# Chunk attention and a multiplicative FFN on one core: q and k of the first two tiles loaded four tokens a partition and transposed by 64 columns

## The chip, the core and the metric

The kernel runs on one core of one Trainium2 chip. TensorE (PE) does matmuls and transposes into PSUM; VectorE (DVE) and ScalarE (ACT) copy and do the softmax; GpSimd (POOL) issues the loads that cast float32 to bf16 on the way; SyncE (SP) issues the transposes by DMA and the transfers of the output. All transfers share 16 DMA engines. The metric is the device time of one execution in microseconds, the median of several runs.

## What is computed

```python
# q, k, v: (8, 8, 576, 64) float32; chunks of 64 tokens, 9 per batch, 8 heads
scores = (1 / sqrt(64)) * matmul(q_c, k_c.transpose(0, 1, 2, 4, 3))   # 64 x 64 in each chunk
attn = exp(scores - scores.max(-1)); attn /= attn.sum(-1) + 1e-9
x = matmul(attn, v_c)                        # heads side by side: (4608, 512)
h = ((x @ w1) * (x @ w2)) @ w3               # d_model 512, d_ff 1024
out = h @ w_out                              # (4608, 512) float32
```

## The kernel before

A group is 128 tokens, two chunks, of all 8 heads; 36 groups make the 4608 tokens. A tile is four groups, 512 tokens; there are nine. w3 and w_out are first multiplied to one matrix, w3o (`add_w3o`: eight times eight transposes, L448, and eight matmuls, L459), so that a tile is x by w1 and w2 (L491), the product of both (DVE, L500), and that by w3o (L522).

A group (`add_group`, L324) goes: load of q and k (`load_qk`, L267: one transfer each, 128 tokens on 128 partitions, 8 heads of 64 numbers, so runs of 256 bytes in HBM and 128 bytes in SBUF); transpose of both, for groups 0 to 11 by eight PE transposes of 128 columns (`t_emit`, L337), for groups 12 to 35 by one DMA transpose (`qk_turn`, L341); copies of k to `kT` and of q to `qd`, whose other half is zero, so that one matmul does two heads (L229 on ACT, L231 on DVE); eight score matmuls (L365) into `p_sc`; maximum, difference, exponential, sum and normalisation (L373, L377, L381, L385, L391); transpose of the result by PE (`at_emit`, L396) or, for groups 16 to 35, by a DMA transpose (`at_turn`, L347); eight matmuls with v (`av_emit`, L407) into `p_av`; a copy into `xt` (`x_copy`), from which L491 reads.

The order of all work is set by `Plan`: every operation is added with its engines, a cost, a key and what it needs, and a list scheduler picks, engine by engine, what is ready with the lowest key. The result is a fixed order for each engine, which the chip then follows; engines wait for one another on semaphores. Where the plan sees PE idle in the beginning, it puts dummy matmuls (`warm`, L585, 14 of them ahead of the first work). Loads are issued by POOL in the order of `LOADS`, then the other groups in turn. A transfer waits until the one eight places before it in its queue has landed. `ident`, which every PE transpose reads, is made by POOL at its place in `LOADS`, after eight loads and the first of the next.

SP issues, in the planned order, four staged rows of w_out, the DMA transposes, and the output: one transfer for each 128 tokens, 256 KB (`o_out`, L532). The output is held back until the loads of group 35 are in (`after=[c] + raws[OUT_AFTER]["ops"]`), with keys from `OUT_KEY` on; until then it lies in `kept`, parts of w3 and w_out that are no longer read, and in 20 buffers `o_sb`. So SP's queue reads, near the end: the DMA transpose of q and k of group 35, four outputs, that of the attention of group 32, eight outputs, group 33, five, group 34, six, group 35, the rest.

Of the kernel before, what the change touches and what calls it, by code (L numbers as in the profile page):

```python
# [10 lines left out]
ACT = mybir.ActivationFunctionType  # L11
# [3 lines left out]

LOADS = [('qk', 0), ('w3', 7, 8), ('w3', 3, 4), ('qk', 1), ('w3', 0, 1), ('wo', 4, 8), ('w3', 1, 2), ('ident',),
         ('qk', 2), ('w3', 2, 3), ('w3', 5, 6), ('qk', 3), ('w3', 6, 7), ('qk', 5), ('qk', 4), ('v', 0, 0, 2), ('w3', 4,
         5), ('w12', 0, 2), ('qk', 6), ('w12', 4, 6), ('qk', 7), ('w12', 2, 4), ('w12', 6, 8), ('qk', 8), ('v', 1, 0, 2),  # L20
         ('qk', 9), ('qk', 10)]
TILES = [4] * 9
XT = 16
STAGED = 4
OUT_AFTER, OUT_KEY = 35, 80
# [134 lines left out]
def kernel(  # L160
# [19 lines left out]
    nc = tc.nc  # L180
    B, H, S, D = q.shape
    C = 64
    NCH = S // C
    N_TOK = B * S
    D_MODEL = H * D
# [9 lines left out]
    bf = mybir.dt.bfloat16  # L195
    f32 = mybir.dt.float32

    BUFS = {"raw": 6, "kqT": 4, "kT": 3, "qd": 3, "vd": 3, "sd": 2, "e": 2, "an": 4, "at": 6, "w3t": 2, "abT": 2,
            "a_sb": 3, "o_sb": 20, "xt": XT, "ffn": 6, "p_sc": 1, "p_av": 1}
# [19 lines left out]

    qds = [wpool.tile([P, 2, NM, 2 * C], bf, tag=f"qd{i}", name=f"qd{i}") for i in range(BUFS["qd"])]  # L220
    vds = [wpool.tile([P, NM, NCH, 2 * D], bf, tag=f"vd{i}", name=f"vd{i}") for i in range(BUFS["vd"])]
    es = [wpool.tile([P, 8, C + 1], bf, tag=f"e{i}", name=f"e{i}") for i in range(BUFS["e"])]
    halves = [slice(0, C), slice(C, P)]

# [25 lines left out]
    def load(cost, issue, emit, **kw):  # L250
        return plan.add("POOL", cost, 0, emit, lag=landing, issue=issue, **kw)

    def chunks(g):
        return [divmod(2 * g + cc, NCH) for cc in range(2)]

    raws, v_got, v_first, w12_got, w3_got, wo_got, wo_cut = {}, {}, {}, {}, {}, [], []

    def load_qk(g):
        (b0, c0), (b1, c1) = chunks(g)
        parts = [(slice(0, P), b0, c0, 2)] if b0 == b1 else [(halves[0], b0, c0, 1), (halves[1], b1, c1, 1)]  # L260
        box = raws[g] = {"ops": []}
        for w, src in enumerate((q, k)):
            for r, b, c, n in parts:
                def emit(eng, w=w, src=src, r=r, b=b, c=c, n=n):
                    if "t" not in box:
                        box["t"] = sb("raw", [P, 2, H, D])
                    nc.gpsimd.dma_start(box["t"][r, w], src[b, :, c * C:(c + n) * C, :].rearrange("h p d -> p h d"))  # L267
                box["ops"].append(load(0.45 * n, 0.5 + 0.2 * n, emit, takes=() if box["ops"] else ("raw",)))

    def load_v(b, y0, y1):  # L270
        for t in range(2):
# [52 lines left out]

    def add_group(g, kt, ks, ka, kv):
        box = {}
        bc = chunks(g)
        qd = qds[g % len(qds)]

        turned = g in QK_BY_DMA  # L330

        def t_emit(eng):
            t = box["tr"] = ps("ffn", [P, 2, NM, P], bf)
# [23 lines left out]
            return emit  # L357

        def s_emit(eng):
            sc = box["sc"] = ps("p_sc", [P, 2, 2, 2, C])  # L360
# [7 lines left out]
        def flat(x):  # L368
            return x.rearrange("p cc y t k -> p (cc y t) k")

        def max_emit(eng):
            nm = box["nm"] = sb("nm", [P, 8, 1], f32, bufs=3)
            nc.vector.tensor_reduce(nm[:, :, 0], flat(box["sc"]), axis=AX.X, op=ALU.max)  # L373

        def sub_emit(eng):
            sd = box["sd"] = sb("sd", [P, 8, C], f32)
            nc.vector.tensor_sub(sd[:], flat(box["sc"]), box["nm"].to_broadcast([P, 8, C]))  # L377

        def exp_emit(eng):
            e = box["e"] = es[g % len(es)]  # L380
# [32 lines left out]
        got = raws[g]["ops"]  # L413
        if turned:
            tr = kc = plan.add("SP", 1.75, kt, qk_turn, after=got, takes=("kqT",), uses=[(got[0], "raw")], lag=3.5, issue=1.3)
            held, cost = [(tr, "kqT")], (0.35, 0.6)
        else:
            tr = plan.add("PE", 0.46, kt, t_emit, after=got + [made_ident], takes=("ffn",), uses=[(got[0], "raw")], lag=0.2)
            held, cost = [(tr, "ffn")], (0.43, 0.66)
            kc = plan.add(("DVE", "ACT"), cost, kt, k_copy, after=(tr,), takes=("kT",), uses=held)  # L420
        q0 = plan.add(("DVE", "ACT"), cost, kt, q_copy(0), after=[tr] + zero_q, takes=("qd",), uses=held)
        q1 = plan.add(("DVE", "ACT"), cost, kt, q_copy(1), after=(tr, q0), uses=held)
        s = plan.add("PE", 0.24, ks, s_emit, after=(kc, q0, q1), takes=("p_sc",), uses=[(kc, "kqT" if turned else "kT"), (q0, "qd")],
                     lag=0.2)
# [10 lines left out]
        av = plan.add("PE", 0.24, kv, av_emit, after=[ac] + [o for b, _ in bc for y_ in (0, 1) for o in v_got[b, y_]], takes=("p_av",),  # L435
                      uses=[(ac, "at")] + [(v_first[b], "vd") for b in sorted({b for b, _ in bc})], lag=0.2)
        x_done[g] = plan.add(("ACT", "DVE"), 0.68, kv, x_copy, after=(av,), takes=("xt",), uses=[(av, "p_av")])


    w3o_done = []  # L440
# [34 lines left out]
    outs = []  # L475
    kept = [w3_sb[:, i:i + 1, :].rearrange("p a n -> p (a n)").bitcast(f32) for i in range(FO)]
    kept += [wo_sb[:, i:i + 2, :].rearrange("p a n -> p (a n)").bitcast(f32) for i in range(0, FO, 2)]

    def add_tile(g0, n, kab, ko_):
        box = {}  # L480
# [32 lines left out]
        for tk, x0, x1 in cols:  # L513
            cuts = (0, FO - 2, FO) if last and not tk else (0, FO)

            def o_mm(i, tk=tk, x0=x0, x1=x1, cuts=cuts):
                def emit(eng):
                    if not i:
                        box["o", tk, x0] = ps("ffn", [P, D_MODEL])
                    t = box["o", tk, x0]  # L520
                    for ki in range(cuts[i], cuts[i + 1]):
                        nc.tensor.matmul(t[:, :x1 - x0], box["abT"][:, ki, tk * P:(tk + 1) * P], w3o_sb[:, ki, x0:x1],  # L522
                                         start=(ki == 0), stop=(ki == FO - 1))
                return emit

            def o_copy(eng, tk=tk, x0=x0, x1=x1):
                box["os", tk, x0] = kept[g0 + tk] if g0 + tk < len(kept) else sb("o_sb", [P, D_MODEL], f32)
                copy(eng, box["os", tk, x0][:, :x1 - x0], box["o", tk, x0][:, :x1 - x0])

            def o_out(eng, tk=tk, x0=x0, x1=x1):  # L530
                r0 = (g0 + tk) * P
                nc.sync.dma_start(out[r0:r0 + P, x0:x1], box["os", tk, x0][:, :x1 - x0])  # L532
# [15 lines left out]
    for what, *args in LOADS:  # L548
        if what == "ident":
            made_ident = plan.add("POOL", 0.6, 0, lambda eng: make_identity(nc, ident[:]), lag=0.3)  # L550
        else:
            {"qk": load_qk, "v": load_v, "w12": load_w12, "w3": load_w3, "wo": load_wo}[what](*args)
    landing = 2.5
    for g in range(NG):
        if g not in raws:
# [62 lines left out]
```

## Time and profile before

Three runs took 251.49, 253.83 and 252.03 us, median 252.03. The profiled execution took 252.69 us by itself, with a span of 250.9 us and a mean granted TensorE clock of 0.993.

| engine | busy us | share | what it does most |
|---|---|---|---|
| PE | 239.3 | 95% | L491 131.6, L522 66.8, L459 15.6 |
| DVE | 173.8 | 69% | L500 48.7, five softmax steps of about 24.5 each |
| ACT | 146.3 | 58% | copies 42.0 (`a_sb`), 22.7 (`qd`), exponential 22.8 |
| POOL | 101.4 | 40% | issue of loads |

The engines' busy times overlap, so they do not add up. The time line of an engine gives the start and length of a run of equal instructions, and in brackets the idle time ahead of it with what ended it. Matmuls are pipelined: the distance from one start to the next says what one costs, not the length. The DMA share in the stretches is per engine and can exceed 1, since several transfers are in flight on an engine. "us to landing" is from the issue of a transfer until its data is in.

### The profile page before, as it was taken

How to read it: one execution, taken by the hardware profiler on the slowest of the kernel's cores; microseconds unless marked ns; L12 is line 12 of the kernel's file. 1: busy time of each engine (PE TensorE's matmuls, PEld its weight loads, DVE VectorE, ACT ScalarE, POOL GpSimd, SP SyncE). 2: the span in 40 equal slices, each digit the busy share in tenths (PEclk: the TensorE clock that was granted, in tenths of full speed). 3: DMA queues.
4: the chain of work that ended last, by engine and by line, in shares of the span. 5: the costliest groups of instructions: out<-in, count | busy, mean ns of one | idle time of the engine just before them, and what ended most of it. 6: DMA issues, size and time to landing. Idle time of an engine off the chain costs nothing.

```text
span 250.9 us, 4671 instructions
## 1 busy us (share of the span) xinstructions
PE 239.3 (95%) x1737; PEld 125.3 (50%) x1769; DVE 173.8 (69%) x315; ACT 146.3 (58%) x250; POOL 101.4 (40%) x127
## 2 busy tenths in 40 slices
PE   8599979998999999999999999999999999999994
PEld 2355755545555555545444545454454444444443
DVE  6176988976888889798778998887898842222310
ACT  8537686566867677667658466655666433433222
POOL 8656869887529764248326331720000000000000
PEclk9799999999999999999999999999999999999999
DMA  6999999999999999999999999999979994121114
GB/s 157 191 195 185 139 176 178 180 147 144 139 120 150 147 155 158 157 134 153 141 131 156 157 139 157 135 154 149 160 119 353 295 340 138 42 84 43 42 44 167
DMA packets 160454, 38.58 MB, mean 154 GB/s; under 512 B 149424, under 2 KB 154416, under 8 KB 160432
## 3 DMA queue, kind: packets, MB, share of 16 engines
q0 software_dynamic: 118160, 18.88, 114.5%
q1 hardware_dynamic: 42272, 19.41, 41.9%
q8 instruction: 14, 0.23, 0.4%
q14 instruction: 8, 0.07, 0.1%
HBM read 38.80 MB, written 9.44 MB: 192 GB/s over the span
## 4 chain that ended last, share of the span: by engine, by line
PE 76%; DMA 16%; POOL 3%; issue 3%; DVE 1%; ACT 1%; POOLq 0%
PE ffn L491 41%; PE ffn L522 23%; DMA vd<-in_v_dram 7%; DMA at<-an 4%; PE p_av L407 3%; PE p_sc L365 3%; DMA raw<-in_q_dram 3%; DMA raw<-in_k_dram 2%; PE ffn L459 2%; PE ffn L337 1%; PE p_av L585 1%; POOL raw L267 1%; POOL vd L273 1%; PE ffn L396 1%; PE ffn L448 1%
## 5 line engine op out<-in xcount | busy, mean ns | idle before, releaser
L491 PE MATMUL ffn<-xt,w_sb 128*128 128x512 bf16 x555 | 131.6, 379 | 1.1
L491 PEld LDWEIGHTS <-w_sb 128*128 128x128 bf16 x576 | 53.9, 98 | 58.3
L500 DVE TENSOR_TENSOR abT<-a_sb,ffn 128x512 bf16<-128x512 f32 x72 | 48.7, 679 | 36.6 <-PE ffn L491 34.8
L522 PE MATMUL ffn<-w3o_sb,abT 128*128 128x512 bf16 (+2 forms) x298 | 66.8, 368 | 0.4
L229 ACT COPY a_sb<-ffn 128x512 f32<-128x512 f32 x72 | 42.0, 583 | 34.1 <-PE ffn L491 33.5
L267 POOL DMA_DIRECT2D raw<-in_q_dram x40 | 34.3, 860 | 33.6 <-DMA kqT<-raw 13.6
L522 PEld LDWEIGHTS <-abT 128*128 128x128 bf16 x304 | 28.1, 98 | 29.6
L267 POOL DMA_DIRECT2D raw<-in_k_dram x40 | 34.1, 852 | 19.3 <-DMA vd<-in_v_dram 9.6
L373 DVE TENSOR_REDUCE nm<-p_sc 128x8 f32<-128x512 f32 x36 | 24.3, 676 | 6.5 <-PE p_sc L365 6.5
L229 ACT COPY o_sb<-ffn 128x512 f32<-128x512 f32 (+2 forms) x20 | 10.8, 542 | 29.4 <-PE ffn L522 29.3
L385 DVE TENSOR_REDUCE ss<-e 128x8 f32<-128x520 bf16 x36 | 24.8, 688 | 3.5 <-ACT e L381 3.3
L381 ACT ACTIVATE e<-sd 128x512 bf16<-128x512 f32 x36 | 22.8, 634 | 3.9 <-DVE sd L377 3.5
L377 DVE TENSOR_TENSOR sd<-p_sc,nm 128x512 f32<-128x512 f32 x36 | 24.5, 681 | 0.5
L391 DVE TENSOR_TENSOR an<-e,rs 128x512 bf16<-128x512 bf16 x36 | 24.6, 684 | 0.2
L229 ACT COPY qd<-kqT 64x512 bf16<-64x512 bf16 x37 | 22.7, 614 | 2.7 <-DMA kqT<-raw 2.4
L229 ACT CAST xt<-p_av 128x512 bf16<-128x512 f32 x27 | 15.8, 586 | 10.1 <-PE p_av L407 9.9
L273 POOL DMA_DIRECT2D vd<-in_v_dram x16 | 18.5, 1162 | 5.7 <-PE ffn L491 2.8
L407 PEld LDWEIGHTS <-vd 128*128 128x128 bf16 x288 | 13.0, 98 | 10.4 <-issue 1.5
L407 PE MATMUL p_av<-at,vd 128*128 128x64 bf16 x288 | 14.4, 193 | 2.4 <-DMA vd<-in_v_dram 1.7
L459 PE MATMUL ffn<-wo_sb,w3t 128*128 128x512 bf16 x60 | 15.6, 379 | 0.6 <-DVE w3t L231 0.4
L365 PEld LDWEIGHTS <-qd 128*128 128x128 bf16 x288 | 12.6, 99 | 5.4 <-DVE qd L231 0.4
L285 POOL DMA_DIRECT2D w_sb<-in_moe_w_dram x16 | 9.9, 629 | 2.2 <-DMA vd<-in_v_dram 0.8
(44 smaller groups left out, 150.9 us busy)
## 6 DMA issues: line engine op xcount, KB each, us to landing
out_dram<-o_sb SPq DMA_DIRECT2D x23, 256.0 KB, 2.4
vd<-in_v_dram POOLq DMA_DIRECT2D x16, 288.0 KB, 9.7
raw<-in_q_dram POOLq DMA_DIRECT2D x32, 128.0 KB, 9.3
raw<-in_k_dram POOLq DMA_DIRECT2D x32, 128.0 KB, 9.3
w_sb<-in_moe_w_dram POOLq DMA_DIRECT2D x8, 256.0 KB, 8.8
w_sb<-in_moe_w_dram POOLq DMA_DIRECT2D x16, 128.0 KB, 5.7
out_dram<-w_sb SPq DMA_DIRECT2D x8, 256.0 KB, 2.5
o_sb<-in_moe_w_out_dram SPq DMA_DIRECT2D x4, 256.0 KB, 3.9
```

The source lines that it names most:

```text
L229: nc.scalar.copy(o, i)
L267: nc.gpsimd.dma_start(box["t"][r, w], src[b, :, c * C:(c + n) * C, :].rearrange("h p d -> p h d"))
L273: nc.gpsimd.dma_start(vds[b % len(vds)][halves[t], 2 * y0:2 * y1, :, t * D:(t + 1) * D].rearrange("p m c d -> p (m c) d"), v[b, NM * t + 2 ...
L373: nc.vector.tensor_reduce(nm[:, :, 0], flat(box["sc"]), axis=AX.X, op=ALU.max)
L377: nc.vector.tensor_sub(sd[:], flat(box["sc"]), box["nm"].to_broadcast([P, 8, C]))
L381: nc.scalar.activation(e[:, :, :C], box["sd"][:], ACT.Exp, scale=scale)
L385: nc.vector.reduce_sum(ss[:], box["e"][:], axis=AX.X)
L391: nc.vector.tensor_mul(an[:], box["e"][:, :, :C], box["rs"].to_broadcast([P, 8, C]))
L407: nc.tensor.matmul(t[:, m, cc, :], vds[b % len(vds)][:, m, c, :], box["at"][:, 2 * cc + y, u * C:(u + 1) * C], start=True, stop=True)
L491: nc.tensor.matmul(t[:, :w], wt[:, ki, j * P:(j + 1) * P], x[:, ki, :], start=(ki == 0), stop=(ki == KO - 1))
L500: nc.vector.tensor_mul(box["abT"][:, j, :w], box["as", j][:, :w], box["b", j][:, :w])
L522: nc.tensor.matmul(t[:, :x1 - x0], box["abT"][:, ki, tk * P:(tk + 1) * P], w3o_sb[:, ki, x0:x1], start=(ki == 0), stop=(ki == FO - 1))
```

## The change

For tiles 0 and 1 (groups 0 to 7, `NQ = 2`) a load now covers 512 tokens of two heads: 4 tokens on each of 128 partitions, so that a run is 1 KB in HBM and 512 bytes in SBUF. A "group" of these tiles is 256 tokens of four heads in place of 128 tokens of eight. Transposes take 64 columns each and put two of them one above the other; the tokens come out ordered by their place in the four. The copies put the keys and queries in that order, the normalisation puts the columns of the attention back to the order of v, and the rows of the output stay permuted until they are stored: the stores of these eight blocks are two each, with 64 partitions, whose rows go to every fourth row of HBM. `LOADS` is reordered, with `ident` behind the first eight loads; `o_sb` goes from 20 to 12 buffers and the eight halves of the new load buffers join `kept`.

In tile 1 each load is cut in two, 16 and 112 partitions, where the batch ends. The diff, cut to its core:

```diff
-LOADS = [('qk', 0), ('w3', 7, 8), ('w3', 3, 4), ('qk', 1), ('w3', 0, 1), ('wo', 4, 8), ('w3', 1, 2), ('ident',), ('qk', 2), ...
+LOADS = [('quad', 0, 0), ('quad', 0, 1), ('ident',), ('w3', 2, 3), ('w3', 5, 6), ('wo', 4, 8), ('w3', 4, 5), ('w3', 3, 4),
+         ('quad', 1, 0), ('w3', 6, 7), ('w3', 7, 8), ('w3', 1, 2), ('v', 0, 0, 2), ('w3', 0, 1), ('quad', 1, 1), ('w12', 0, 2), ...
+NQ = 2
...
+    def load_quad(n, y):
+        box = quads[n, y] = {"ops": []}
+        c0 = 8 * n
+        cut = min(8, (c0 // NCH + 1) * NCH - c0)
+        parts = [(c0, 0, cut)] + ([(c0, cut, 8)] if cut < 8 else [])
+        for w, src in ((1, k), (0, q)):
+            for t in range(2):
+                for c, i0, i1 in parts:
...
+                        h = NM * t + 2 * y
+                        nc.gpsimd.dma_start(box["t"][i0 * C // R:i1 * C // R, w, t],
+                                            src[b, h:h + 2, c * C:(c + i1 - i0) * C, :].rearrange("h (p r) d -> p h (r d)", r=R))
...
+        def quad_turn(w):
+            def emit(eng):
+                tr = raw["tr", w] = ps("ffn", [P, 2, 8 * C], bf)
+                for t in range(2):
+                    for i in range(R):
+                        for u in range(2):
+                            nc.tensor.transpose(tr[halves[u], t, i * P:(i + 1) * P], raw["t"][:, w, t, u, i * D:(i + 1) * D], ident[:])
...
+        def quad_k(eng):
+            box["kT"] = sb("kT", [P, NM, P]).rearrange("p (s a) c -> p s (a c)", s=2)
+            copy(eng, box["kT"].rearrange("p s (cc r k) -> p s cc r k", cc=4, r=R),
+                 raw["tr", 1].rearrange("p s (r h cc k) -> p h s cc r k", r=R, h=2, cc=4)[:, hf])
...
         def norm_emit(eng):
             an = box["an"] = sb("an", [P, 8, C])
-            nc.vector.tensor_mul(an[:], box["e"][:, :, :C], box["rs"].to_broadcast([P, 8, C]))
+            if quad:
+                nc.vector.tensor_mul(an.rearrange("p x (k r) -> p x k r", r=R), box["e"][:, :, :C].rearrange("p x (r k) -> p x k r", r=R),
+                                     box["rs"].to_broadcast([P, 8, C]).rearrange("p x (k r) -> p x k r", r=R))
...
             def o_out(eng, tk=tk, x0=x0, x1=x1):
                 r0 = (g0 + tk) * P
-                nc.sync.dma_start(out[r0:r0 + P, x0:x1], box["os", tk, x0][:, :x1 - x0])
+                if g0 + tk >= 4 * NQ:
+                    nc.sync.dma_start(out[r0:r0 + P, x0:x1], box["os", tk, x0][:, :x1 - x0])
+                else:
+                    for i in range(2):
+                        nc.sync.dma_start(out[r0 + i * C:r0 + (i + 1) * C].rearrange("(k r) n -> r k n", r=R),
+                                          box["os", tk, x0][halves[i], :])
```

The order of the instructions, which can be read from the built program without running it, has PE with 128 transposes of 64 columns (16 at a time) where 64 of 128 columns were, and 23 dummy matmuls in place of 25. SP's queue near the end reads: the DMA transpose of group 35, eight of the 64-partition outputs, the attention of group 32, the other eight, three outputs of 256 KB, group 33, seven, group 34, six, group 35, the rest.

More of the change, by code (lines that the diff above doesn't have):

```diff
@@ L13 @@
 ALU = mybir.AluOpType
[L18 to L21, printed above, removed]
+LOADS = [('quad', 0, 0), ('quad', 0, 1), ('ident',), ('w3', 2, 3), ('w3', 5, 6), ('wo', 4, 8), ('w3', 4, 5), ('w3', 3, 4), ('quad', 1, 0), ('w3', 6, 7), ('w3', 7, 8), ('w3', 1, 2), ('v', 0, 0, 2), ('w3', 0, 1), ('quad', 1, 1), ('w12', 0, 2), ('w12', 2, 4), ('qk', 8), ('w12', 6, 8), ('w12', 4, 6), ('v', 1, 0, 2), ('qk', 9), ('qk', 10)]
 TILES = [4] * 9
+NQ = 2
 XT = 16
@@ L182 @@
     C = 64
+    R = 4
     NCH = S // C
@@ L196 @@
     f32 = mybir.dt.float32
-    BUFS = {"raw": 6, "kqT": 4, "kT": 3, "qd": 3, "vd": 3, "sd": 2, "e": 2, "an": 4, "at": 6, "w3t": 2, "abT": 2,
-            "a_sb": 3, "o_sb": 20, "xt": XT, "ffn": 6, "p_sc": 1, "p_av": 1}
+    BUFS = {"raw": 6, "rawq": 4, "kqT": 4, "kT": 3, "qd": 3, "vd": 3, "sd": 2, "e": 2, "an": 4, "at": 6, "w3t": 2, "abT": 2,
+            "a_sb": 3, "o_sb": 12, "xt": XT, "ffn": 6, "p_sc": 1, "p_av": 1}
     consts = ctx.enter_context(tc.tile_pool(name="consts", bufs=1))
@@ L221 @@
     vds = [wpool.tile([P, NM, NCH, 2 * D], bf, tag=f"vd{i}", name=f"vd{i}") for i in range(BUFS["vd"])]
+    rawqs = [wpool.tile([P, 2, 2, 2, R * D], bf, tag=f"rawq{i}", name=f"rawq{i}") for i in range(BUFS["rawq"])]
     es = [wpool.tile([P, 8, C + 1], bf, tag=f"e{i}", name=f"e{i}") for i in range(BUFS["e"])]
@@ L268, in load_qk, with emit @@
                 box["ops"].append(load(0.45 * n, 0.5 + 0.2 * n, emit, takes=() if box["ops"] else ("raw",)))
+    quads, turned_in = {}, []
+    def load_quad(n, y):
[6 more added lines that the diff above has]
+                for c, i0, i1 in parts:
+                    def emit(eng, w=w, src=src, t=t, i0=i0, i1=i1):
+                        if "t" not in box:
+                            box["t"] = rawqs[len(turned_in) % len(rawqs)]
+                            turned_in.append(box)
+                        b, c = divmod(c0 + i0, NCH)
+                        h = NM * t + 2 * y
+                        nc.gpsimd.dma_start(box["t"][i0 * C // R:i1 * C // R, w, t],
+                                            src[b, h:h + 2, c * C:(c + i1 - i0) * C, :].rearrange("h (p r) d -> p h (r d)", r=R))
+                    box["ops"].append(load(0.088 * (i1 - i0), 0.5 + 0.02 * (i1 - i0), emit, takes=() if box["ops"] else ("rawq",)))
     def load_v(b, y0, y1):
@@ L359, in s_emit @@
         def s_emit(eng):
-            sc = box["sc"] = ps("p_sc", [P, 2, 2, 2, C])
+            sc = ps("p_sc", [P, 2, 2, 2, C])
+            box["sc"] = sc.rearrange("p cc y t k -> p (cc y t) k")
             for cc in range(2):
@@ L411, in x_copy @@
             copy(eng, xt[:, :, g % XT * P:(g % XT + 1) * P], box["av"].rearrange("p m cc t -> p m (cc t)"))
-        got = raws[g]["ops"]
-        if turned:
+        emits = (k_copy, q_copy, s_emit, av_emit, x_copy)
+        cost = (0.43, 0.66)
+        if quad:
+            emits = (quad_k, quad_q, quad_s, quad_av, quad_x)
+            got = raw["ops"]
+            if not hf:
+                raw["turns"] = [plan.add("PE", 0.48, kt, quad_turn(w), after=got[:len(got) // (1 + w)] + [made_ident],
+                                         takes=("ffn",), uses=[(got[0], "rawq")], lag=0.2) for w in (1, 0)]
+            trk, tr = raw["turns"]
+            held = [(tr, "ffn")]
+            kc = plan.add(("DVE", "ACT"), cost, kt, emits[0], after=(trk,), takes=("kT",), uses=[(trk, "ffn")])
+        elif turned:
+            got = raws[g]["ops"]
             tr = kc = plan.add("SP", 1.75, kt, qk_turn, after=got, takes=("kqT",), uses=[(got[0], "raw")], lag=3.5, issue=1.3)
@@ L417, in add_group @@
         else:
+            got = raws[g]["ops"]
             tr = plan.add("PE", 0.46, kt, t_emit, after=got + [made_ident], takes=("ffn",), uses=[(got[0], "raw")], lag=0.2)
[L419 to L424, printed above, removed]
+            held = [(tr, "ffn")]
+            kc = plan.add(("DVE", "ACT"), cost, kt, emits[0], after=(tr,), takes=("kT",), uses=held)
+        q0 = plan.add(("DVE", "ACT"), cost, kt, emits[1](0), after=[tr] + zero_q, takes=("qd",), uses=held)
+        q1 = plan.add(("DVE", "ACT"), cost, kt, emits[1](1), after=(tr, q0), uses=held)
+        s = plan.add("PE", 0.24, ks, emits[2], after=(kc, q0, q1), takes=("p_sc",),
+                     uses=[(kc, "kqT" if turned else "kT"), (q0, "qd")], lag=0.2)
         mx = plan.add("DVE", 0.69, ks, max_emit, after=(s,), lag=0.05)
@@ L434, in add_group @@
             ac = plan.add(("DVE", "ACT"), (0.43, 0.66), ka, at_copy, after=(at,), takes=("at",), uses=[(at, "ffn")])
-        av = plan.add("PE", 0.24, kv, av_emit, after=[ac] + [o for b, _ in bc for y_ in (0, 1) for o in v_got[b, y_]], takes=("p_av",),
+        av = plan.add("PE", 0.24, kv, emits[3], after=[ac] + [o for b, _ in bc for y_ in ((y,) if quad else (0, 1)) for o in v_got[b, y_]], takes=("p_av",),
                       uses=[(ac, "at")] + [(v_first[b], "vd") for b in sorted({b for b, _ in bc})], lag=0.2)
-        x_done[g] = plan.add(("ACT", "DVE"), 0.68, kv, x_copy, after=(av,), takes=("xt",), uses=[(av, "p_av")])
+        x_done[g] = plan.add(("ACT", "DVE"), 0.68, kv, emits[4], after=(av,), takes=("xt",), uses=[(av, "p_av")])
     w3o_done = []
@@ L477 @@
     kept += [wo_sb[:, i:i + 2, :].rearrange("p a n -> p (a n)").bitcast(f32) for i in range(0, FO, 2)]
+    kept += [t[:, i].rearrange("p a b c -> p (a b c)").bitcast(f32) for t in rawqs for i in range(2)]
     def add_tile(g0, n, kab, ko_):
@@ L551 @@
         else:
-            {"qk": load_qk, "v": load_v, "w12": load_w12, "w3": load_w3, "wo": load_wo}[what](*args)
+            {"qk": load_qk, "quad": load_quad, "v": load_v, "w12": load_w12, "w3": load_w3, "wo": load_wo}[what](*args)
     landing = 2.5
     for g in range(NG):
-        if g not in raws:
+        if g >= 4 * NQ and g not in raws:
             load_qk(g)
```

36 lines of the change are left out of this document (31 added, 5 removed).

## The prediction, on record before the run

> **What bounds the kernel now.** I read the busy line over the span first, then the chain that ended last, PE's time line at both ends, POOL's loads, and last SP's queue around 184 to 206 us.
>
> ```profile
> PE   8599979998999999999999999999999999999994
> PEclk9799999999999999999999999999999999999999
> DMA  6999999999999999999999999999979994121114
> GB/s 157 191 195 185 139 176 178 180 147 144 139 120 150 147 155 158 157 134 153 141 131 156 157 139 157 135 154 149 160 119 353 295 340 138 42 84 43 42 44 167
> ```
>
> PE is the bound from about 21 us on. It is short of work only in the first slices, and cold in the second. The DMA engines are full too, until slice 30; then the output held back goes out at 300 to 380 GB/s and they fall idle.
>
> ```profile
> 9.58 0.80 PE L337 MATMUL ffn<-ident,raw 128*128 128x128 bf16 x8 [2.62 <-POOL ident masks.py:199]
> 10.27 1.03 PE L448 MATMUL ffn<-ident,w_sb 128*128 128x128 bf16 x8
> ...
> 11.95 1.06 PE L448 MATMUL ffn<-ident,w_sb 128*128 128x128 bf16 x8
> ...
> 20.88 0.61 PE L337 MATMUL ffn<-ident,raw 128*128 128x128 bf16 x8
> 21.33 1.89 PE L459 MATMUL ffn<-wo_sb,w3t 128*128 128x512 bf16 x8
> ...
> 34.40 0.39 PE L407 MATMUL p_av<-at,vd 128*128 128x64 bf16 x8 [0.37 <-DMA vd<-in_v_dram]
> ...
> 57.54 0.29 PE L407 MATMUL p_av<-at,vd 128*128 128x64 bf16 x4 [1.30 <-DMA vd<-in_v_dram]
> ```
>
> To see: the first real work starts at 9.58, 2.62 us idle ahead of it, waiting for `ident`; after that the clock is granted 0.50 from 10 to 13 us, so the eight transposes at 11.95 take 0.86 to the next start, where the eight at 20.88 take 0.45. So a transpose costs 56 ns warm, 107 cold. Other starts give 216 ns for 512 columns and 29 ns for 64. Counting PE's order with these, 231.3 us of work lie behind 10.27, and the last matmul ends at 247.6: 6.1 us are lost on the way (1.7 to the clock, about 2.5 to v and its copies, the rest spread).
>
> ```profile
> raw<-in_q_dram POOLq DMA_DIRECT2D x32, 128.0 KB, 9.3
> w_sb<-in_moe_w_dram POOLq DMA_DIRECT2D x16, 128.0 KB, 5.7
> ```
>
> Landings one by one: behind a full queue a q or k load of 128 KB takes 0.87 us (58.2, 59.1, 59.9), a w1/w2 load of the same size, whose runs are 1 KB as the new ones are, comes every 0.65 us, as fast as POOL issues it (629 ns against 860).
>
> ```profile
> 184.95 1.23 SPq L341 DMA_TRANSPOSE kqT<-raw  x1
> 186.24 2.04 SPq L532 DMA_DIRECT2D out_dram<-w_sb  x4
> 188.38 1.32 SPq L347 DMA_TRANSPOSE at<-an  x1
> 189.75 2.10 SPq L532 DMA_DIRECT2D out_dram<-w_sb  x4
> 191.89 2.98 SPq L532 DMA_DIRECT2D out_dram<-wo_sb  x4
> 194.97 1.96 SPq L347 DMA_TRANSPOSE at<-an  x1
> ```
>
> ```profile
> 194.62 0.40 PE L407 MATMUL p_av<-at,vd 128*128 128x64 bf16 x8
> ```
>
> The last k load, issued at 165.17, lands 19.7 us later; that lets SP issue the transpose of group 35, and behind it stand outputs and the attention transposes of groups 32 to 35 in one queue. Four outputs take 2.1 us to issue, and 0.68 us each at 381 GB/s (204 to 206 us). Group 32's transpose, issued at 188.38, lands 3.1 us later at 191.5; PE needs it at 194.6. Group 33's lands at 199.1 for 202.0. The slack is 3 us.
>
> **The change, part by part.** *Start.* POOL's eight loads at 0.63 us from 1.25 end at 6.3, and `ident` (8.94 to 9.54 before, 0.6) is made by 6.9 with no wait. The first k, two transfers, was in by 8.96 together with the first q; at 0.65 in place of 0.87 it is in by about 8.4. So PE starts about 1 us sooner. But all eight loads (2 MB) now stand ahead of the first w3: 8.4 and six more at 0.65 make 12.3, and w3 itself 1.25, as the w3 loads landed before (10.2, 11.45): 13.5; at the earliest 12.2 if the first pair lands with `ident`. I take 13.0, against 10.27. In this time PE does 64 transposes and two groups' scores, which before came later. Counted from the new order, 229.6 us lie behind that point, against 231.3 before: 2.7 - 1.7 = +1.0 us.
>
> *Transposes.* That count has the 64-column transposes at 56 ns. No row shows one; the nearest rows are L337 (56 ns, 107 cold) and, for half the width, L365's 29 ns. The first 64 run while loads are awaited. For the other 64 the bounds are -1.7 and +3.3 us; I take 56, since the 128 columns that are streamed are the same.
>
> *Waits regained.* Twelve loads ahead of the first v cost 0.22 less, 2.6 us, less some 0.5 for the four that are split off with 16 partitions: v lands near 32 in place of 34.3, while PE comes to it at 13.0 + 17.7 = 30.7. Some of the 2.5 lost to v remains. The cold stretch goes if PE has no idle 2.6 us: 0 to 1.7 gained. I take 1.5 for both, range 0 to 2.7.
>
> *Copies and normalisation.* Same counts of elements, in runs of 16, or with a step of 16 in the normalisation. L391 takes 684 ns now, the rate of the float32 steps, so I take nothing for it; the spread between DVE's copies of 512 elements (0.42 bf16, 0.69 float32) bounds it at 0.4 us more for each of eight groups, and as much for the 24 copies: at most 6 us of DVE, of which PE would see part (DVE is busy 4.8 of 5 us from 25 to 30). Front end together: +1.0 - 1.5 = -0.5 us, between -4 and +5.
>
> *The outputs.* Eight transfers of 256 KB become sixteen of 128 KB: half of one is 0.34 us on all engines. But their HBM side now counts 4 by 16 by 512, where each transfer of the trace begins with a count of 64 or 128. The packets of the output queue are whole lines of the pattern (7534 of 7538 under 8 KB, 2 KB rows); I read this as lines dealt to the engines by the outermost count, and 4 is dealt to 4 engines. Bounds: 0.34 us if all 16 still carry it, four times as much, 1.36, if four do. The second is the nearer to the form of the instruction, and I take it. The Trainium skill (DMA: Bandwidth & Descriptors, "Why a DMA increments its semaphore by 16 and not by 1") states that a transfer runs on the largest number up to 16 that divides the outermost counts of both sides, here 4 of 64 and 4; by it the sum is the one below, with 0.34 it is the first rival's, and no run here shows it yet.
>
> All these stand in SP's one queue ahead of the attention transposes, each engine working in order. Loads end some 2 us sooner (sixteen times 0.22 less eight small transfers), so the first output is issued at 184.2; 0.5 to issue and 1.3 until data flows (a lone output lands in 2.4 to 2.6, 0.68 of it data); 8 x 1.36; the transpose about 0.9 behind: group 32 lands at 197.8. PE comes to it at 194.6 - 0.5 = 194.1: 3.7 us idle. Then eight more (10.9) and three of 0.68: group 33 lands at 197.8 + 10.9 + 2.0 + 0.9 = 211.6, while PE, 5.6 us of work later by its new order, is there at 203.4: 8.2 us idle. Group 34: seven at 0.68 and 0.9 more, 217.3, for PE at 217.0: 0.3. Group 35 comes in time (222.3 for 222.7). An idle 8.2 us costs the clock: as 10 to 13.5 us shows, 3.4 us at half, 1.7. Sum: -0.5 + 3.7 + 8.2 + 0.3 + 1.7 = +13.4. The profiled execution, 252.69, becomes 266.1; it stood 0.66 above the median, 252.03, so I forecast 265.
>
> What PE gains in the beginning is worth nothing in this case: the end is set by group 33's landing plus the 47.3 us of PE work behind it. That landing moves with the loads' end (2 us sooner or later) and the price of one output; at 1.13 a transfer in place of 1.36 it comes 3.7 us sooner. Own range 258 to 269.
>
> **The rivals.** *All 16 engines carry the new outputs.* For it: nothing but that the bytes are the same. Then SP's issue is the limit, 0.52 each: group 32 issued at 184.2 + 8 x 0.52 = 188.4 and landed at 191.5, in time; group 33 eleven later, 195.5, landed at 199.6 for PE at 199.7, just in time. The front end alone is left: 252.03 - 0.5, about 251.5 (249.5 to 254).
>
> *Faster: the same, and transposes in pairs.* If two 64-column transposes, one above the other, run together at L365's 29 ns, 1.7 us go, and the whole cold stretch another 1.7: 251.5 - 3.4 = 248.1. It decides only if the outputs do not hold up group 32 and 33, that is below some 0.6 us each. The Trainium skill (TensorE: Matmul & The Clock Gate, "Part 3: Packing small matmuls") says that matmuls on separate column strips overlap, which would give this pairing; here no trace shows it.
>
> *Slower by DVE.* The stepped normalisation and the short runs cost the bounds above and PE waits for attention in the first 60 us: 251.5 + 4.5 = 256. Against it: L391 is already at one element a step.
>
> **How the numbers follow.** Four engines 0.65, around 265; sixteen 0.13, around 251.5; pairs 0.16, around 248; DVE 0.06, around 256. Within 1% (249.5 to 254.5, about what a measurement of this kernel tells from no change) is the first rival: 0.13. Faster 0.16, slower 0.65 + 0.06 = 0.71. The range, 249.5 to 269, leaves out the pairs and a little above: 0.2.
>
> **What would show it.** Outputs of 128 KB whose landing grows from 2.5 to some 10 us while the DMA share falls to about a quarter between 184 and 200 us; PE idle ahead of the attention matmuls of groups 32 and 33, released by `at<-an`; a low clock behind. In the front: first transposes near 8.4, the first w3 transposes near 13, v waits under 2.5 us, starts of the 64-column transposes 56 ns apart. I am wrong if those outputs land in 2.5 us, or if the idle before group 33 stays under 3 us.

## The result, and the profile after

The changed kernel took 271.56 us, the median of 4 runs (269.55 to 272.81), beside 251.76 us for the kernel before (4 runs, 251.3 to 253.83): a ratio of 1.0762, interval 1.0664 to 1.086. Here and below, a ratio and its interval leave out runs in a slower state, which the medians and ranges include. The profiled execution of the changed kernel took 269.55 us, with a span of 267.8 and a mean granted clock of 0.975; it is the fastest of its four. Against the profiled 252.69 of before that is 16.9 us more.

The page of the changed kernel, the same slices as before:

```profile
PE   8789887999999999999999999999928279999995
PEclk9999999999999999999999999999986869999999
DMA  7999999999999999999999999999372999112114
GB/s 195 200 196 134 168 111 151 174 154 151 156 141 146 156 145 118 156 151 141 157 157 136 156 140 157 145 146 111 89 107 89 202 301 333 39 39 77 43 39 157
```

The slices are 6.7 us. In slices 28 to 30 (from 187 us) the DMA engines carry 89 to 107 GB/s; the kernel before had three slices there at 295 to 353; PE has two holes, in slices 29 and 31, and the clock falls after each. The GB/s of slices 3 to 6 (20 to 47 us) is lower too.

SP's time line near the end:

```profile
185.18 1.23 SPq L404 DMA_TRANSPOSE kqT<-raw  x1
186.47 6.90 SPq L614 DMA_DIRECT2D out_dram<-w_sb  x8
193.48 2.24 SPq L410 DMA_TRANSPOSE at<-an  x1
195.76 9.76 SPq L614 DMA_DIRECT2D out_dram<-w_sb  x8
205.56 2.35 SPq L611 DMA_DIRECT2D out_dram<-wo_sb  x3
208.02 4.11 SPq L410 DMA_TRANSPOSE at<-an  x1
```

The two runs of eight are the outputs of 64 partitions. Group 32's transpose is issued at 193.5 and group 33's at 208.0, against 188.38 and 194.97 before. What the DMA engines do meanwhile, and the clock (columns: busy time and instructions of each engine, granted clock, DMA share, GB/s):

```profile
190.00:192.00 2.00, 2.00 (x25) 1.15 (x23) 1.58 (x4) 1.92 (x4) 0.00 (x0) 1.00 0.26 83
192.00:194.00 2.00, 2.00 (x11) 0.89 (x10) 0.62 (x2) 1.29 (x3) 0.00 (x0) 1.00 0.27 85
...
198.00:200.00 2.00, 0.00 (x0) 0.00 (x0) 0.00 (x0) 0.00 (x0) 0.00 (x0) 0.55 0.26 93
200.00:204.00 4.00, 2.29 (x20) 1.44 (x21) 1.18 (x2) 0.59 (x1) 0.00 (x0) 0.50 0.28 79
...
212.00:218.00 6.00, 2.36 (x13) 1.16 (x14) 0.00 (x0) 0.59 (x1) 0.00 (x0) 0.50 1.03 261
```

A share of 0.26 is what four busy engines of sixteen would show; the trace does not name the engines. At 84 GB/s one output of 128 KB takes 1.56 us. PE's time line, at both ends:

```profile
7.71 0.65 PE L363 MATMUL ffn<-ident,rawq 128*64 128x128 bf16 x16 [0.45 <-POOL ident masks.py:199]
8.29 0.60 PE L668 MATMUL p_av<-zeros 128*128 128x512 bf16 x2
...
14.09 0.61 PE L525 MATMUL ffn<-ident,w_sb 128*128 128x128 bf16 x8
...
34.34 0.39 PE L388 MATMUL p_av<-at,vd 128*128 128x64 bf16 x8 [1.01 <-DMA vd<-in_v_dram]
...
41.44 1.03 PE L569 MATMUL ffn<-xt,w_sb 128*128 128x512 bf16 x4
44.20 1.89 PE L569 MATMUL ffn<-xt,w_sb 128*128 128x512 bf16 x8 [1.73 <-DMA w_sb<-in_moe_w_dram]
...
201.71 0.61 PE L472 MATMUL p_av<-at,vd 128*128 128x64 bf16 x8 [5.61 <-DMA at<-an]
...
215.64 0.61 PE L472 MATMUL p_av<-at,vd 128*128 128x64 bf16 x8 [6.53 <-DMA at<-an]
```

From these the 16.84 us by which PE's last matmul ends later come out in full. Without its wait PE would have been at group 32's attention matmul at 201.71 - 5.61 = 196.10, where it was at 194.62 before: +1.48 from all that lies ahead. Then it waits 5.61 and 6.53, both released by the DMA transpose: 12.14. Behind each wait the clock stands at 0.5 for some 3 to 4 us, which costs 1.76 and 1.47 against the same work at full clock: 3.23. The sum is 16.85; nothing is left over.

In front, the first real work comes at 7.71, not at 9.58, and the clock stays at 1.00. But tile 0 reaches its first matmul by w1 and w2 at 41.44, against 39.07 before, and after four of them waits 1.73 us for w1 and w2.

### The profile page after: what moved, and what is told of

Same layout as the page of the kernel before. It is cut to its first block, busy times and chain, and to the rows that moved or that the text cites. A ratio compares the mean times of both kernels' runs of the same rounds, so it can differ in the third digit from the quotient of the medians.

```text
span 267.8 us, 4863 instructions
## 1 busy us (share of the span) xinstructions
PE 244.9 (91%) x1831; PEld 124.8 (47%) x1831; DVE 173.8 (65%) x310; ACT 149.4 (56%) x255; POOL 101.5 (38%) x133
## 4 chain that ended last, share of the span: by engine, by line
PE 75%; DMA 16%; POOL 7%; issue 1%; ACT 0%; POOLq 0%
PE ffn L569 43%; PE ffn L600 24%; DMA w_sb<-in_moe_w_dram 8%; DMA at<-an 6%; PE p_av L472 3%; PE p_sc L429 3%; POOL rawq L286 2%; DMA raw<-in_k_dram 2%; POOL w_sb L305 2%; POOL w_sb L314 1%; POOL vd L293 1%; PE ffn L461 1%; PE ffn L400 1%; PE p_av L388 0%; ACT o_sb L229 0%
## 5 line engine op out<-in xcount | busy, mean ns | idle before, releaser
L569 PE MATMUL ffn<-xt,w_sb 128*128 128x512 bf16 x576 | 134.1, 379 | 1.7 <-DMA w_sb<-in_moe_w_dram 1.7
L600 PE MATMUL ffn<-w3o_sb,abT 128*128 128x512 bf16 (+2 forms) x304 | 70.1, 378 | 0.0
L267 POOL DMA_DIRECT2D raw<-in_q_dram x31 | 26.6, 860 | 28.9 <-DMA kqT<-raw 11.5
L267 POOL DMA_DIRECT2D raw<-in_k_dram x31 | 26.6, 862 | 18.3 <-DMA vd<-in_v_dram 12.0
L472 PE MATMUL p_av<-at,vd 128*128 128x64 bf16 x224 | 11.5, 196 | 12.1 <-DMA at<-an 12.1
L229 ACT COPY qd<-kqT 64x512 bf16<-64x512 bf16 x34 | 20.9, 615 | 1.5 <-DMA kqT<-raw 1.2
L456 DVE TENSOR_TENSOR an<-e,rs 128x512 bf16<-128x512 bf16 x28 | 19.2, 684 | 0.2
L472 PEld LDWEIGHTS <-vd 128*128 128x128 bf16 x224 | 10.4, 100 | 18.8 <-DMA at<-an 13.1
L429 PEld LDWEIGHTS <-qd 128*128 128x128 bf16 x224 | 9.9, 99 | 4.0
L286 POOL DMA_DIRECT2D rawq<-in_q_dram x12 | 7.6, 632 | 9.1 <-DMA vd<-in_v_dram 3.7
```

The lines of the kernel that those rows point to most:

```text
L229: nc.scalar.copy(o, i)
L472: nc.tensor.matmul(t[:, m, cc, :], vds[b % len(vds)][:, m, c, :], box["at"][:, 2 * cc + y, u * C:(u + 1) * C], start=True, stop=True)
L569: nc.tensor.matmul(t[:, :w], wt[:, ki, j * P:(j + 1) * P], x[:, ki, :], start=(ki == 0), stop=(ki == KO - 1))
```

## The experiments

Two theories stood after the result. *Engines:* the outputs of 64 partitions run on four DMA engines, because the outermost count of their HBM side is 4, and hold up the attention transposes behind them in SP's queue. *Count:* it is the sixteen issues in place of eight that hold up the queue, whatever the engines. Beside them stood the front end, of which the profile did not say whether the transposes, the normalisation or the loads made it late.

**The stores alone, on the kernel before.** Four kernels are the kernel before with nothing changed but the outputs of the first eight blocks, two each of 64 partitions. They differ in the HBM side: 4 x 16 rows as in the change, 8 x 8, 16 x 4, and 64 rows in one run. (The rows of these blocks land in another order in the first three.)

```diff
-                nc.sync.dma_start(out[r0:r0 + P, x0:x1], box["os", tk, x0][:, :x1 - x0])
+                if g0 + tk >= 8:
+                    nc.sync.dma_start(out[r0:r0 + P, x0:x1], box["os", tk, x0][:, :x1 - x0])
+                else:
+                    for i in range(2):
+                        nc.sync.dma_start(out[r0 + i * C:r0 + (i + 1) * C].rearrange("(k r) n -> r k n", r=4),   # or 8, 16; or plain
+                                          box["os", tk, x0][halves[i], :])
```

Expected of count 4: 

> The kernel before, with only the output of the first eight blocks stored as the change does: sixteen transfers of 64 partitions whose rows are dealt out with an outermost count of 4 in HBM (the rows then stand in the wrong order; nothing else is touched). Theory (a transfer runs on as many DMA engines as its outermost count, and the attention transposes of groups 32 and 33 wait behind it): from the trace of the changed kernel 15.0 us from the first of these outputs to the landing of group 32, then 14.6 us to that of group 33 with one more transfer of 256 KB between; PE idle 6.8 and 5.7 us, 3 us lost to the clock, about 267 us. Rival (the new loads and the front end make the loss): 252 us.

Expected of count 8: 

> As with 4, with an outermost count of 8. Theory: 0.78 us for each of these outputs in place of 1.56, the DMA share near 0.5 between 188 and 194 us; PE idle about 0.6 us ahead of group 32 and 2.5 ahead of group 33, 255 to 257 us. Rival (rows scattered over HBM are slow whatever the count): as slow as with 4, 267 us. Rival (front end): 252 us.

Expected of count 16: 

> As with 4, with an outermost count of 16. Theory: all 16 engines work, SP's issue of 0.52 us each is the limit, group 33 lands near 201.2 for PE at 202.0: no idle, 252 us within 1. Rival (scattered rows): 267 us. Rival (twice as many transfers): above 255 us.

Expected of 64 rows in one run: 

> The kernel before, with the output of the first eight blocks stored in two halves of 64 partitions each, in plain order (outermost count 64). Theory: as with 16, 252 us within 1. Rival (twice as many transfers, half the size): above 255 us.

| outermost count | us, median (range) | ratio (interval) | DMA share, GB/s at 190 to 192 us |
|---|---|---|---|
| 4 | 268.71 (267.02 to 270.19) | 1.0643 (1.0579 to 1.0707) | 0.25, 66 |
| 8 | 257.43 (255.05 to 257.57) | 1.0176 (1.012 to 1.0233) | 0.48, 137 |
| 16 | 257.4 (255.09 to 258.91) | 1.0167 (1.0102 to 1.0231) | 0.59, 203 |
| 64 | 255.83 (253.01 to 259.14) | 1.0117 (1.0078 to 1.0155) | 0.94, 207 |

With count 4 PE shows the two waits of the changed kernel again:

```profile
201.53 0.61 PE L407 MATMUL p_av<-at,vd 128*128 128x64 bf16 x8 [7.06 <-DMA at<-an]
215.99 0.61 PE L407 MATMUL p_av<-at,vd 128*128 128x64 bf16 x8 [5.42 <-DMA at<-an]
```

The form of the store alone makes 16 of the 20 us. From 4 to 8 the share doubles and 11 us go: the engines' theory holds for the large part. Rows scattered over HBM are not the cause, since 8 and 16 scatter them too. Count 8 came out just above its 255 to 257 us, with PE waits of 1.07 and 2.21 us where 0.6 and 2.5 were expected. But from 8 to 16 nothing more goes, and with 16 and 64 the time does not come back to 252, as both were expected to: a miss. SP's queue with 64 rows in one run:

```profile
187.18 5.07 SPq L536 DMA_DIRECT2D out_dram<-w_sb  x8
192.34 1.25 SPq L347 DMA_TRANSPOSE at<-an  x1
193.64 5.78 SPq L536 DMA_DIRECT2D out_dram<-w_sb  x8
199.46 2.07 SPq L533 DMA_DIRECT2D out_dram<-wo_sb  x4
201.63 1.59 SPq L347 DMA_TRANSPOSE at<-an  x1
```

SP issues without a pause, 0.63 to 0.72 us for each, where the first eight outputs of 256 KB took 2.04 and 2.10 us for four before, 0.52 each. The data does not hold it up: the halves land 2.4 us (median) after their issue, first and last alike. So sixteen halves take 10.9 us of the queue and eight wholes 4.1, and group 33's transpose comes 6.7 us later than before (0.9 of it because the first output did), more than its slack: PE waits 2.81 us for it. The count's theory is right for the remaining 1.2 to 1.8%; why a half takes longer to issue than a whole stays open.

**The changed kernel with the stores taken out of the way.** First the sixteen halves ordered behind group 35's attention transpose:

```diff
-        plan.add("SP", 0.7, max(c.key, OUT_KEY + i), emit, after=[c] + raws[OUT_AFTER]["ops"],
+        plan.add("SP", 0.7, max(c.key, OUT_KEY + i), emit, after=[c] + raws[OUT_AFTER]["ops"] + ([last_at[0]] if i < 4 * NQ else []),
```

> The changed kernel, with the sixteen stores of count 4 ordered behind the attention transpose of group 35. Theory (the loss is the place in the queue, not the stores): they take some 25 us on four engines from about 207 us on, beside PE, and the end is not touched: 253 to 255 us. Rival (four slow engines hold up every output to the end): the last outputs land late, above 260 us.

It took 256.43 us (254.26 to 258.3), 1.0185 (1.0126 to 1.0244), above the 253 to 255 of the theory and far below the rival's 260. No wait for an attention transpose is left on PE. What the stores cost by standing ahead of the attention transposes is thus some 14.5 us (1.0762 less 1.0185, of 252). A remainder of 4.7 is left.

Then the stores as before, whole, with the permutation undone elsewhere: the copies of the queries put them back in natural order.

```diff
-                     raw["tr", 0][halves[u]].rearrange("p t (r h cc k) -> p h t cc r k", r=R, h=2, cc=4)[:, hf])
+                copy(eng, qd[halves[u], :, u * C:(u + 1) * C].rearrange("p (cc t) (k r) -> p t cc r k", t=2, r=R), ...)
```

> The changed kernel, with the queries put back in their own order in the copies (stride of four on the write) so that the output leaves in whole rows by 128 partitions as before. Theory (the stores make the loss): the two waits of 5.6 and 6.5 us and the 3.2 us of clock go; what is left is the front end, which brought PE to group 32 1.5 us later than before: 253 to 255 us. Rival (the new front end costs much more than that shows): above 257 us. Rival (the front end gains and was only hidden): under 250 us.

It took 261.58 us (259.38 to 262.84), 1.0403 (1.0353 to 1.0452): a miss, though not by the front end that the rival has. The groups of the copies to `qd` from PSUM, first of the changed kernel, then of this one (x count | busy, mean ns | idle ahead of them):

```profile
L229 ACT COPY qd<-ffn 64x512 bf16<-64x512 bf16 x14 | 7.9, 580 | 2.7 <-DVE qd L231 1.6 <-PE ffn L363 1.0
L231 DVE COPY qd<-ffn 64x512 bf16<-64x512 bf16 x10 | 4.1, 418 | 2.2 <-ACT kT L229 1.1 <-ACT qd L229 1.0
```

```profile
L229 ACT COPY qd<-ffn 64x512 bf16<-64x512 bf16 x14 | 13.5, 998 | 8.2 <-DVE qd L231 7.0 <-PE ffn L363 1.2
L231 DVE COPY qd<-ffn 64x512 bf16<-64x512 bf16 x10 | 11.0, 1114 | 3.9 <-ACT qd L229 3.7 <-ACT kT L229 0.2
```

The same 512 elements take about twice as long or more when they are written with a step of four. PE then waits 4.9 us for `qd` on ACT and 1.4 on DVE. The kernel with whole stores below differs from this one in nothing but these copies and stands at 1.0116 in place of 1.0403. Two kernels more were built on this one and can't tell what they were made for, for the same reason. Only tile 0 changed (`NQ = 1`): 

> As the version with natural query order, with only the first tile loaded and transposed in the new way (NQ = 1): no load is split in two. Theory (the front end lost because sixteen small transfers count in the eight that may be in flight): PE keeps its warm clock and its start at 7.7 us, and the waits for w1/w2 and v shrink: 249 to 252 us. Rival (the layout itself costs, by the normalisation at 1018 ns in place of 684 and the copies): 253 us or more.

It took 257.66 us (257.33 to 258.18), 1.0249 (1.0212 to 1.0286), not the 249 to 252 of the theory, with 4.0 us of PE waiting for `qd`. And tile 1's loads in one piece (see below for the edit): 

> As the version with natural query order, but the loads of tile 1 are not split where the batch ends: eight transfers of 128 partitions in place of sixteen (they fetch other tokens, chunks 0 to 7 of batch 1, so two chunks are wrong; bytes and work stay). Theory (the number of transfers in flight limits the front end): POOL's waits of 2.9 us near 15 and 30 us go, first tile matmul at 39 us or sooner, 1.5 to 2.5 us faster than with the split. Rival (bytes limit it): the same time as with the split.

It took 261.48 us (259.86 to 262.33), 1.0392 (1.0348 to 1.0436), no different from 261.58; PE waits for the copies either way.

**The front end by itself.** The next kernels keep the copies of the change. The first has whole stores, so that the rows of the first eight blocks stay permuted and nothing of the stores' change is left:

```diff
-                if g0 + tk >= 4 * NQ:
-                    nc.sync.dma_start(out[r0:r0 + P, x0:x1], box["os", tk, x0][:, :x1 - x0])
-                else:
-                    for i in range(2): ...
+                nc.sync.dma_start(out[r0:r0 + P, x0:x1], box["os", tk, x0][:, :x1 - x0])
```

> The changed kernel, but each output is one transfer of 128 partitions as before (the first eight blocks' rows stay in the permuted order). Nothing of the stores is left of the change. If the 4.6 us that the late stores still cost against before come from the front end: 255 to 256 us, with the first matmul of tile 0 by w1 and w2 at 41 us or later (before 39.07). If they come from the eight extra transfers at the end: 252 us. No wait of the attention's matmul for its transpose after group 31 in either.

It took 256.1 us (254.61 to 257.51), 1.0116 (1.007 to 1.0163), and tile 0 reaches w1 and w2 at 46.15: the front end, not the late stores, is the larger part of what remains. The second adds one edit, tile 1's loads in one piece:

```diff
-        parts = [(c0, 0, cut)] + ([(c0, cut, 8)] if cut < 8 else [])
+        parts = [(c0, 0, 8)]
...
-                        b, c = divmod(c0 + i0, NCH)
+                        b, c = n, 0
```

> As the kernel with whole stores, and the loads of tile 1 are one transfer each in place of two (tile 1 reads other tokens: batch 1's first 512). If it is the eight extra transfers that keep GpSimd's queue waiting for landings (waits of 2.95 and 2.98 us there at 18 and 33 us) and so the loads of v and w1, w2 late: 252 to 253.5 us, the waits for v and w1, w2 gone. If it is the order of the loads or the normalisation: as the kernel with whole stores.

It took 251.14 us (250.23 to 255.36), 0.9955 (0.9924 to 0.9986), less than the 252 to 253.5 expected. One edit to eight loads takes back 1.6%, 4.0 us, and PE's time line shows no wait for v, w3, w1 or w2 any more. Tile 0 reaches w1 and w2 at 40.46, still later than the 39.07 of before, in a kernel that is no slower: this time alone does not say what the front end costs, for the order of PE's work differs. POOL's time line shows how, with whole stores first, then with tile 1 in one piece (L286 issues the new loads, L305 those of w1 and w2):

```profile
35.72 0.66 POOL L286 DMA_DIRECT2D rawq<-in_q_dram  x1 [3.62 <-DMA vd<-in_v_dram]
37.63 0.50 POOL L286 DMA_DIRECT2D rawq<-in_q_dram  x1 [1.25 <-DMA vd<-in_v_dram]
38.32 0.66 POOL L286 DMA_DIRECT2D rawq<-in_q_dram  x1 [0.18 <-issue]
38.98 4.92 POOL L305 DMA_DIRECT2D w_sb<-in_moe_w_dram  x8
```

```profile
26.03 1.48 POOL L286 DMA_DIRECT2D rawq<-in_q_dram  x2
28.05 0.62 POOL L305 DMA_DIRECT2D w_sb<-in_moe_w_dram  x1 [0.55 <-DMA w_sb<-in_moe_w_dram]
31.67 0.61 POOL L305 DMA_DIRECT2D w_sb<-in_moe_w_dram  x1 [2.99 <-DMA vd<-in_v_dram]
```

Both wait 3 us or more for the first v to land: a transfer is not issued until the one eight places before it is in. What stands behind that wait differs. In the one it is pieces of the new loads, among them some of 16 KB, and w1 and w2 come at 38.98; in the other w1 and w2 begin at 28.05. The stretch from 15 to 45 us of the kernel with the split, the GB/s in 40 slices and issue to landing, and then the GB/s with tile 1 in one piece:

```profile
GB/s 193 202 231 202 199 192 190 122 122 81 15 89 171 191 93 137 145 156 163 160 154 147 131 151 178 192 178 166 63 78 121 27 22 119 124 136 170 98 111 102
...
rawq<-in_q_dram POOLq DMA_DIRECT2D x4, 16.0 KB, 5.3
rawq<-in_k_dram POOLq DMA_DIRECT2D x2, 16.0 KB, 10.9
```

```profile
GB/s 210 203 228 198 214 196 189 194 197 216 199 214 216 197 169 160 153 142 144 188 140 167 181 195 193 188 167 163 166 169 186 175 201 154 155 152 158 172 171 180
```

16 KB take 5.3 to 10.9 us to land, and hold their place in the eight for that long; a whole load takes 9.8 to 9.9 us in the other kernel. The engines run dry, to 15 and 22 GB/s, at 22.5 and 39 us; with the loads in one piece the same stretch never falls below 140. That it is the number of the pieces that costs, and not that some are 16 partitions small, is read from POOL's waits; no run has as many pieces in another form.

Third, the change for tile 0 alone, with the eight half stores behind group 35:

```diff
-NQ = 2
+NQ = 1
-... ('quad', 1, 0), ('w3', 6, 7), ... ('quad', 1, 1), ('w12', 0, 2), ...
+... ('qk', 4), ('qk', 5), ('w3', 6, 7), ... ('qk', 6), ('qk', 7), ('w12', 0, 2), ...
```

> The change for tile 0 alone, tile 1 loaded as before, with contiguous copies of the queries, and the eight half stores behind the transpose of group 35. If the front end's loss lies in tile 1's loads: 252 to 254 us. If it lies in tile 0's transposes, copies and normalisation: 255 to 256 us, as with both tiles.

It took 253.83 us (250.87 to 258.8); by the ratio, 1.0007 (0.9969 to 1.0044), there is no difference from before. The twelve runs spread widely, and seven of them make the ratio, so this is the weakest of the three. As far as it goes, tile 0's part of the change, late half stores included, costs nothing and brings nothing; that the front end's loss is tile 1's split rests on the second kernel.

Last, the cold clock in the kernel before, by 25 dummy matmuls in front in place of 14:

```diff
-        fills, last, cold = 14, 0.0, True
+        fills, last, cold = 25, 0.0, True
```

> The kernel before with 25 dummy matmuls in front in place of 14, so that PE is busy until the identity is there (9.4 us). If PE's granted clock fell to 0.5 at 10 to 12 us because of the 2.62 us of idle time, it stays at 1.00 there, the transposes of w3 come about 0.9 us sooner, and the whole takes 250.5 to 251.5 us. If the loads set the front end: 252 us, the saved time lost again in waits for v and w1, w2.

It took 251.63 us (250.01 to 253.42), 0.9965 (0.9934 to 0.9995). The stretches from 8 to 12 us of this kernel:

```profile
8.00:10.00 2.00, 0.66 (x9) 0.53 (x8) 0.00 (x0) 0.23 (x1) 1.70 (x4) 1.00 1.28 194
10.00:12.00 2.00, 1.71 (x26) 1.22 (x26) 1.01 (x2) 1.17 (x2) 1.49 (x3) 1.00 2.04 176
```

The clock stays at 1.00 where it was 0.50, with 1.34 us of idle time left in place of 2.62. The cold stretch had been reckoned at 1.7 us; 0.9 (0.35% of 252) came out at the end. That it came from the clock is not shown: of the 28 runs of the kernel before that it is compared with, five had a mean granted clock of 0.998 or more without it, and they are no faster (median 252.95) than the others (252.26). Nor do these runs settle how long an idle time the clock bears. In the kernel with tile 1 in one piece it fell to 0.50 behind idle times of 1.33 and 0.44 us; in that with tile 0 alone it stayed at 1.00 behind 1.74. The warm start is the one version with the reference's rows in place that beats both kernels, and barely. A version with whole first loads, late half stores and a warm start was not built: the parts, 0.9955 for the loads and some 0.7% back for the late stores (1.0185 against 1.0116, intervals that overlap), would put it within 0.5% of the kernel before, which is an estimate.

## Why the prediction was right or wrong

The direction, the place and the mechanism were right: slower, by outputs on four DMA engines that hold up groups 32 and 33 in SP's queue. The size was too small: 265 forecast, 271.56 measured, above the upper end of the range, 269. Against the profiled 269.55, the sum of 266.1 lacks 3.5 us; the other 2.0 us lie between that execution and the median.

The step that failed is the landing of group 33, in the term of the outputs. The prediction says itself that the end is set by this landing and the work behind it. It came at 215.6, not at 211.6, 4.0 us late: the loads did not end sooner, so that the first output was issued at 186.47 and not at 184.2 (2.3 us), and an output took 1.56 us and not 1.36 (1.4 us more up to group 32). Behind it 0.3 us of idle time ahead of group 34 and 0.2 of the clock did not come: 3.5. Counted along PE instead, as the prediction adds up, the same 3.5 us stand in the first two terms below (2.0 and 1.5). But what PE lost ahead of group 32, and to the clock behind its first wait, it would else have spent waiting for group 33.

*Start and waits regained* (-0.5 forecast, +1.5 in the profile). PE did start sooner, at 7.71, earlier than the 8.4 of the forecast; the first w3 transposes came at 14.09 for 13.0. "Less some 0.5 for the four that are split off with 16 partitions" is too little: loading tile 1 in one piece is worth 4.0 us, by POOL's waits because the pieces take places among the eight transfers in flight. The cold stretch went, as forecast, in the profile of the changed kernel, but not always: in the kernels with late and with whole stores the first transposes waited for the loads until 8.18 and 8.26, and the clock fell to 0.62 and 0.52 from 10 to 14 us in the former and to 0.68 and 0.50 in the latter. This may be why the profiled execution is the fastest of its four. The two slowest, 272.6 and 272.81 us, have a lower mean clock (0.973 and 0.969, against 0.975 in the other two), which fits in part; more is not on record of them.

*The clock* (1.7 forecast, 3.2 measured). One cold stretch was counted, behind the wait for group 33. There are two: the wait for group 32 was long enough, 5.61 us, to bring its own.

*The outputs.* The idle time was forecast as 3.7 + 8.2 + 0.3 = 12.2 and is 5.61 + 6.53 = 12.14. That agrees by two errors that cancel. "Loads end some 2 us sooner" failed: the last of them landed at 185.05, as before (184.85), and the first output was issued at 186.47, not 184.2. The split is what ate the gain, as SP's time line shows with whole stores, first split, then in one piece:

```profile
188.23 2.43 SPq L404 DMA_TRANSPOSE kqT<-raw  x1
```

```profile
181.01 1.23 SPq L404 DMA_TRANSPOSE kqT<-raw  x1
```

This is the transpose of q and k of group 35; the first output follows it, at 182.29 in the second. And one output took 1.56 us, not 1.36: a quarter of the engines carried 84 GB/s, less than a quarter of the 381 that had been measured on sixteen. Group 32 landed some 3.7 us later than forecast (201.5 for 197.8), group 33 some 4 (215.6 for 211.6), while PE came later too (196.1 for 194.1 and 209.1 for 203.4). The interval between them, 13.9 us, was forecast as 13.8. The rule that the Trainium skill gives (DMA: Bandwidth & Descriptors, "Why a DMA increments its semaphore by 16 and not by 1") agrees with the shares here: 0.26 with an outermost count of 4, 0.48 with 8.

*Copies and normalisation* (0 forecast). The copies of the change are what they were, 418 and 580 ns. The stepped normalisation is not free:

```profile
L456 DVE TENSOR_TENSOR an<-e,rs 128x512 bf16<-128x512 bf16 x28 | 19.2, 684 | 0.2
L453 DVE TENSOR_TENSOR an<-e,rs 128x512 bf16<-128x512 bf16 x8 | 8.1, 1018 | 0.0
```

"The rate of the float32 steps, so I take nothing for it" failed by 334 ns for each of eight groups, within its bound of 0.4; but it stays hidden, for the kernel with tile 1 in one piece has it and takes 0.9955.

*Transposes* (56 ns forecast, bounds 29 and 107). Sixteen take from 7.71 to 8.29, 36 ns each. That is the mechanism of the rival with pairs, near its price of 29. The Trainium skill's statement on column strips (TensorE: Matmul & The Clock Gate, "Part 3: Packing small matmuls") agrees with the trace in kind: two of them cost 73 ns together, where one transpose that streams as many columns costs 56. Against the forecast's count this saves 1.3 us on the 64 transposes that do not run while loads are awaited. Against the kernel before it saves nothing on the transposes themselves: 128 at 36 ns are 4.6 us, 64 at 56 ns were 3.6. It was not tried by itself.

*The first rival* had sixteen engines at 251.5. With sixteen engines and as many outputs the kernel before takes 255.8 to 257.4: its price of 0.52 us an issue was that of whole outputs, and a half takes 0.63 to 0.72.

## What to carry to other kernels

Look at the outermost count of both sides of every transfer that a change of layout touches, and at what stands behind it in the same queue: here a store of 4 x 16 rows took 1.56 us, where one of the same size with a count of 16 or 64 went out every 0.63 to 0.79 us, and the transposes queued behind it made PE wait 12 us. Count transfers and not bytes where a queue holds only so many in flight or issues one after the other: eight pieces of 16 KB cost 4.0 us ahead, eight more outputs 3 to 5 us at the end. Try each place where a permutation can be put by itself: in the normalisation it stayed hidden, in a copy that writes with a step it doubled the copy and PE waited for it.

## What the runs showed of the hardware that was not expected

- DMA transfers of 64 partitions with an outermost count of 4 ran at a share of 0.25 to 0.27 and 72 to 88 GB/s over 5 to 8 us, with 8 at 0.48 and 137 to 164 GB/s; 16 gave 0.59 to 0.71 and 64 gave 0.94, at the same 197 to 210 GB/s.
- An output of 64 partitions took 0.63 to 0.72 us to issue (0.79 in one group of eight with count 16), one of 128 partitions 0.51 to 0.59 in four groups of the kernel before and 0.75 in one.
- Copies of bf16 that write with a step of four elements: 998 ns on ACT and 1114 ns on DVE, against 580 and 418; a multiplication that reads one operand with a step of 16 elements, in runs of four: 1018 ns against 684.
- Two 64-column transposes one above the other: 73 ns, against 56 for one of 128 columns.
- The granted clock fell to 0.50 behind idle times of 1.33 and 0.44 us in one execution and stayed at 1.00 behind 1.34 and 1.74 us in two others.
